# A gated MLP behind an attention block: float16 operands made ahead on GpSimd, and the gate in one pass

## The chip, the cores and the metric

The kernel runs on one core of a Trainium2 chip. The core has a matrix engine (TensorE, PE in the profile), three engines for element-wise work (VectorE, DVE; ScalarE, ACT; GpSimd, POOL), and SyncE (SP), which here does nothing but issue DMA transfers. TensorE reads its operands from the on-chip memory SBUF and writes to the accumulation memory PSUM. Each engine takes its instructions in the order in which they are queued, and semaphores make an instruction wait for work on other engines. The metric is the device time of one execution in microseconds (us).

## The reference

The input x has 2048 rows of 512 float32 numbers. First comes attention with 32 heads of 16 columns, then a gated MLP in which a 2048 x 2048 matrix mixes the rows:

```python
h  = x + softmax_attention(layernorm(x) @ wqkv) @ wo      # 32 heads, 16 columns each
z  = gelu_tanh(layernorm(h) @ w_in)                       # 2048 x 1376
z1 = z[:, :688]
z2 = layernorm(z[:, 688:])                                # 2048 x 688
g  = w_sp @ z2 + b_sp[:, None]                            # w_sp: 2048 x 2048
out = h + (z1 * g) @ w_out                                # w_out: 688 x 512
```

Everything is float32. The kernel keeps the accuracy by splitting an operand into a high part and a low part (the rest) and by multiplying high x high, high x low and low x high: three matmuls for one, in the helper `mm3` (lines 93 to 96).

## The kernel before

The work has four stages, one after another.

*Start.* Rows of x are normalized, turned, and multiplied by wqkv; q, k and v go to DRAM, q and k as float16 parts.

*Attention.* The loop runs over 512 units (group of four heads, block of 512 queries, block of 128 keys), two units an iteration. For each iteration TensorE makes the scores (line 660), ScalarE takes their exponential (L663), and TensorE multiplies by v (L671). So that the exponential does not overflow, the largest score of every query is found ahead: `max_pair` (lines 192 to 239) makes the scores of 128 queries a second time, eight steps an iteration, and VectorE takes their maximum (L215, L224). Eight iterations make a group g; at its end VectorE joins the maxima (nm, L230), GpSimd splits them into two parts (L233 to L235), and in the next iteration VectorE turns them (`max_rows`, L246), after which SP writes them into the query tile as extra rows. The group is needed by the scores some four iterations after its end. GpSimd also clears a part of the tile mx for each group (L203), copies v (L170), and splits wo and w_in into parts (`load_weights`, six times).

*z stage.* For 16 blocks of 128 rows, in the order 0, 1, 8, 9, 2, 10, 3, 11 and so on, so that a row block of the top half is followed by its partner of the bottom half: the attention's output o times 1/sum (GpSimd, L600), times wo (`make_h`), layernorm, turn (`turn`, L843), times w_in in four tiles of 344 columns with twelve matmuls each (`make_z`), gelu (L858), layernorm of the right half (`gate_z`, L864 to L888). All these operands are float32 parts.

*Gate stage.* w_sp @ z2 is done by Strassen's scheme in Winograd's form: w_sp is cut into four quarters a11, a12, a21, a22, z2 into b11, b12 (top rows, left and right columns) and b21, b22; seven products of sums of quarters (s1 to s4, t1 to t3, n4) replace eight. Each product takes, for one block p of 128 rows out of eight, 8 x 3 = 24 matmuls of 344 columns. It runs in two passes over p. The first pass (four products: s3 x t3, s2 x t2, a22 x n4, s1 x t1) loads w_sp, makes the sums on VectorE (`difference`, `sums`) and the parts on ScalarE and VectorE (`put`, L788 and L789), and sends results to DRAM (g_scr). Then b21 and b22 take the place of t2 and t3. The second pass makes the other three (a11 x b11, s4 x b22, a12 x b21), adds the stored results and the bias (L1153), multiplies by z1, turns the product (`Out.turn`, L1117) and multiplies it by w_out, whose 688 rows are five blocks of 128 and one of 48: 18 matmuls of 512 columns for each 128 rows of the output.

The order of instructions on each engine is that of the program text inside `manual_schedule`; in attention GpSimd is not in that list, and a planner places its instructions. SP's queue is one line of DMA issues for all loads and for most stores.

Of the kernel before, what the change touches and what calls it, by code (L numbers as in the profile page):

```python
# [12 lines left out]
I32 = mybir.dt.int32  # L13
# [31 lines left out]
EIGHT_OVER = float(257 << 23)  # L45


@with_exitstack
def block_kernel(ctx: ExitStack, tc: tile.TileContext, x, wqkv, wo, w_in, w_sp4, b_sp, w_out, out):
# [29 lines left out]
    z_scr = [dram.tile([S, FH], F32, name=f"z{i}_scr") for i in range(2)]  # L79
    s_scr = dram.tile([HB, P, HB, P], F32, name="s_scr")  # L80
    g_scr = [dram.tile([3, P, FC], F32, name=f"g{p}_scr") for p in range(HB)]

    def split(hi, lo, src, eh=None, el=None):

        if eh == "act":
            nc.scalar.activation(hi, src, AF.Copy)  # L86
        elif eh == "pool":
            nc.gpsimd.tensor_copy(hi, src)
        else:
            nc.vector.tensor_copy(hi, src)  # L90
        (nc.gpsimd if el == "pool" else nc.vector).tensor_sub(lo, src, hi.bitcast(F32))

    def mm3(ps, lh, ll, rh, rl, first, last):
        nc.tensor.matmul(ps, lh, rh, start=first, stop=False)  # L94
        nc.tensor.matmul(ps, lh, rl, start=False, stop=False)  # L95
        nc.tensor.matmul(ps, ll, rh, start=False, stop=last)  # L96

    def rstd_of(pool, var, n, between=lambda: None):

        hv = pool.tile([P, n], F32, name=f"rs_v{n}")  # L100
        nc.vector.tensor_scalar(hv, var, EPS, 0.5, op0=ALU.add, op1=ALU.mult)
# [62 lines left out]
    def load_v(hg):  # L164
# [5 lines left out]
        nc.gpsimd.tensor_copy(  # L170
# [84 lines left out]
    with ExitStack() as pre:  # L255
# [190 lines left out]
        with tc.manual_schedule(engines={E.PE, E.Activation, E.DVE, E.SP}):  # L446
# [95 lines left out]
            for j in range(24):  # L542
# [18 lines left out]
                if j == 4:  # L561
                    load_v(0)
# [19 lines left out]
    wi2 = [ec.tile([P, DB, 2 * FH], F32R, name=f"wi{i}") for i in range(2)]  # L582
# [36 lines left out]
    def scale_h(sb):  # L619
        mv = e2.tile([P, 2], F32, name="mv")  # L620
        nc.vector.bn_aggr(mv, hst.pop(sb))
        return mv, rstd_of(e2, mv[:, 1:2], 1)
# [19 lines left out]
    with ExitStack() as at:  # L642
# [44 lines left out]
        def load_weights(i):  # L687

            t = wc.tile([P, DB * D], F32, name="wg", tag="w0")
            if i < 2:  # L690
                t = t[:, :2 * D].rearrange("p (a c) -> p a c", a=2)
                a, f = slice(2 * i, 2 * i + 2), slice(0, D)
                src, dst = wo4, wo2
            else:
                t = t[:, :2 * FH].rearrange("p (a c) -> p a c", a=2)
                b = FH * (i // 4)
                a, f = slice(i % 2 * 2, i % 2 * 2 + 2), slice(b, b + FH)
                src, dst = wi4, wi2
            nc.sync.dma_start(t, src[:, a, f])
            split(dst[0][:, a, f], dst[1][:, a, f], t, "pool", "pool")  # L700
# [3 lines left out]
        with tc.manual_schedule(engines={E.PE, E.Activation, E.DVE, E.SP}):  # L704
            for n in range(0, len(units), 2):
                (hg, qb, kb), (_, _, kb1) = units[n:n + 2]
                if hg + 1 < HG and n % 64 < 24 and n % 4 == 0:
# [3 lines left out]
                if hg + 1 < HG and n % 64 == 30:  # L711
                    load_v(hg + 1)
# [36 lines left out]
                if n % 32 == 16 and n < 6 * 32:  # L749
                    load_weights(n // 32)  # L750
# [19 lines left out]
    T = {n: [zc.tile([P, HB, FC], F32R, name=f"{n}_{i}") for i in range(2)]  # L770
         for n in ("t3", "t2", "n4", "t1")}
    QB = HB // 2

    class Slot:


        def __init__(self, pool, tag):
            self.pool, self.tag = pool, tag

        def take(self):  # L780
            t = self.pool.tile([P, 2, HB, P], F32R, name="ws", tag=self.tag)
            return t[:, 0], t[:, 1]

    def parts(hi, lo, src, el=None, eh=None):
        if eh == "pool":
            nc.gpsimd.tensor_copy(hi, src)
        else:
            nc.scalar.activation(hi, src, AF.Copy)  # L788
        (nc.gpsimd if el == "pool" else nc.vector).tensor_sub(lo, src, hi.bitcast(F32))  # L789

    def load_a(halves, i, j, p):

# [434 lines left out]
```

## Time and profile before

| | |
|---|---|
| time, median of 3 runs | 1839.71 us (1837.95 to 1841.82) |
| profiled execution | 1840.91 us, span 1839.0 us |
| TensorE clock granted, mean | 0.995 |
| busy: PE, DVE, ACT, POOL | 97%, 84%, 72%, 11% of the span |
| attention, to its last score product | about 1350 us |
| z stage | about 1356 to 1528 us |
| gate stage | 1528 to 1839 us |

The profile's page gives sums over the whole span; stretches of time, groups of equal instructions and single instructions are read from the trace. In a row of a group, the part after the first bar is the busy time in us and the mean duration of one instruction in ns; after the second bar stands how long the engine had been idle before such instructions and what ended that. In a row of the timeline the first number is the start in us, the second the duration. A name such as `g<-t,ws` is the tile written and the tiles read. PEld is the loading of a matmul's stationary operand.

### The profile page before, as it was taken

How to read it: one execution, taken by the hardware profiler on the slowest of the kernel's cores; microseconds unless marked ns; L12 is line 12 of the kernel's file. 1: busy time of each engine (PE TensorE's matmuls, PEld its weight loads, DVE VectorE, ACT ScalarE, POOL GpSimd, SP SyncE). 2: the span in 40 equal slices, each digit the busy share in tenths (PEclk: the TensorE clock that was granted, in tenths of full speed). 3: DMA queues.
4: the chain of work that ended last, by engine and by line, in shares of the span. 5: the costliest groups of instructions: out<-in, count | busy, mean ns of one | idle time of the engine just before them, and what ended most of it. 6: DMA issues, size and time to landing. Idle time of an engine off the chain costs nothing.

```text
span 1839.0 us, 32468 instructions
## 1 busy us (share of the span) xinstructions
PE 1787.3 (97%) x11616; PEld 857.3 (47%) x11616; DVE 1552.4 (84%) x3137; ACT 1332.4 (72%) x1733; POOL 210.1 (11%) x322
## 2 busy tenths in 40 slices
PE   8999999999999999999999999999989999999999
PEld 6766222222222222222222222222259998998887
DVE  6578999999999999999999999999447778776554
ACT  3333999999999999999999999999954434343221
POOL 2121001011010000000000000000005551001121
PEclk9999999999999999999999999999999999999999
DMA  5343110120021001001011011000135555567551
GB/s 170 118 120 100 41 23 20 28 45 24 22 46 30 22 17 22 23 22 21 14 32 21 9 30 28 9 9 8 45 88 166 165 167 191 185 211 235 177 181 69
DMA packets 148105, 135.90 MB, mean 74 GB/s; under 512 B 62952, under 2 KB 108088, under 8 KB 147944
## 3 DMA queue, kind: packets, MB, share of 16 engines
q1 hardware_dynamic: 143304, 122.56, 23.9%
q10 hardware_dynamic: 4608, 11.27, 1.6%
q8 instruction: 91, 1.49, 0.3%
q14 instruction: 70, 0.57, 0.1%
q0 software_dynamic: 32, 0.01, 0.0%
HBM read 87.01 MB, written 46.17 MB: 72 GB/s over the span
## 4 chain that ended last, share of the span: by engine, by line
PE 67%; ACT 18%; issue 9%; DVE 4%; DMA 2%; SPq 0%; ACTq 0%; POOL 0%; DVEq 0%; POOLq 0%
PE pv L671 18%; PE m L210 13%; ACT pt L663 12%; PE s L660 6%; PE acc L94 6%; PE acc L96 6%; PE acc L95 6%; ACT ab L220 5%; PE g L94 3%; PE g L96 3%; PE g L95 3%; DVE mx L215 1%; PE tp L1117 1%; DMA rc<-r_scr 0%; DMA b<-z_scr 0%
## 5 line engine op out<-in xcount | busy, mean ns | idle before, releaser
L663 ACT ACTIVATE pt<-s 128x1024 f32<-128x1024 f32 x1024 | 996.3, 1038 | 72.3 <-PE s L660 68.8
L215 DVE TENSOR_REDUCE mx<-m 128x1 f32<-128x512 f32 x1511 | 965.5, 684 | 26.3 <-PE m L210 10.2
L671 PE MATMUL pv<-pt,vst 128*32 128x512 f32 x4096 | 551.9, 605 | 0.8 <-ACT o L678 0.8
L210 PE MATMUL m<-kst,qst 48*128 48x512 f16 x1511 | 479.4, 379 | 18.8
L660 PE MATMUL s<-qst,kst 50*128 50x512 f16 x2048 | 418.2, 379 | 2.0 <-DVE mx L215 0.6
L210 PEld LDWEIGHTS <-qst 48*128 48x128 f16 x2048 | 147.2, 94 | 538.9 <-issue 504.6
L660 PEld LDWEIGHTS <-kst 50*128 50x128 f16 x2048 | 144.2, 94 | 150.7 <-issue 73.3
L210 PE MATMUL m<-uvs,qst 48*128 48x512 f16 x503 | 191.3, 381 | 0.0
L224 DVE CUSTOM_DVE_ANT_0 ab<-m,ab 128x512 f32<-128x512 f32 x252 | 171.6, 681 | 3.4 <-ACT ab L220 2.7
L671 PEld LDWEIGHTS pv<-pt,vst 128*32 128x32 f32 x4096 | 83.1, 108 | 182.9 <-issue 167.7
L220 ACT ACTIVATE ab<-m 128x512 f32<-128x512 f32 x251 | 151.6, 604 | 14.4 <-PE tp L210 9.9
L233 POOL TENSOR_SCALAR nm<-nm 128x16 f32<-128x16 f32 x32 | 6.5, 204 | 842.9 <-DVE nm L230 842.9
L788 ACT ACTIVATE ws<-a 128x512 fp32r<-128x512 f32 x80 | 45.8, 621 | 57.7 <-issue 37.9
L94 PE MATMUL acc<-wi,hT 128*128 128x344 f32 x256 | 83.1, 325 | 0.0
L96 PE MATMUL acc<-wi,hT 128*128 128x344 f32 x256 | 81.8, 320 | 0.0
L95 PE MATMUL acc<-wi,hT 128*128 128x344 f32 x256 | 81.7, 319 | 0.0
L858 ACT ACTIVATE z<-acc 128x344 f32<-128x344 f32 x64 | 28.8, 456 | 55.9 <-PE acc L96 55.8
L789 DVE TENSOR_TENSOR ws<-a,ws 128x512 fp32r<-128x512 f32 x80 | 56.8, 751 | 10.2 <-ACT ws L788 10.1
L94 PE MATMUL g<-b,ws 128*128 128x344 f32 x192 | 65.0, 339 | 0.0
L86 ACT ACTIVATE pT<-tp 128x384 fp32r<-128x384 f32 (+2 forms) x48 | 18.3, 382 | 64.4 <-PE tp L1117 47.2
L94 PE MATMUL g<-t,ws 128*128 128x344 f32 x192 | 61.6, 321 | 3.3 <-ACT p L1034 2.0
L95 PE MATMUL g<-b,ws 128*128 128x344 f32 x192 | 61.9, 322 | 0.0
(197 smaller groups left out, 2163.8 us busy)
## 6 DMA issues: line engine op xcount, KB each, us to landing
a<-in_w_sp SPq DMA_DIRECT2D x80, 256.0 KB
z_scr<-z ACTq DMA_DIRECT2D x32, 344.0 KB
qst<-q_scr SPq DMA_DIRECT2D x192, 32.0 KB
kst<-k_scr SPq DMA_DIRECT2D x48, 128.0 KB
z<-z_scr SPq DMA_DIRECT2D x14, 344.0 KB
b<-z_scr SPq DMA_DIRECT2D x24, 172.0 KB
g_scr<-q SPq DMA_DIRECT2D x24, 172.0 KB
xg<-in_x SPq DMA_DIRECT2D x16, 256.0 KB
```

The source lines that it names most:

```text
L94: nc.tensor.matmul(ps, lh, rh, start=first, stop=False)
L95: nc.tensor.matmul(ps, lh, rl, start=False, stop=False)
L96: nc.tensor.matmul(ps, ll, rh, start=False, stop=last)
L210: nc.tensor.matmul(acc, q[r, p, c], keys[r, p], start=True, stop=True)
L215: nc.vector.reduce_max(at(t, e if t else e - 1), acc, axis=AX.X)
L220: nc.scalar.activation(ab[0], acc, AF.Abs)
L224: nc.vector.tensor_tensor_reduce(ab[0], acc, ab[0], 0.5, LOW, ALU.add, ALU.max, at(0, 0))
L660: nc.tensor.matmul(s[:, t, :], k[r, p, kb * P:(kb + 1) * P], q[r, p, :], start=True, stop=True)
L663: nc.scalar.activation(t, s, AF.Exp, scale=scales_[hg // 2])
L671: nc.tensor.matmul(pv[0][32 * j:32 * j + 32, :], vst[hg % 2][:, c:c + 32], pts[j % 2][:, j // 2, :], start=kb == 0, stop=kb == NB - 1)
L788: nc.scalar.activation(hi, src, AF.Copy)
L789: (nc.gpsimd if el == "pool" else nc.vector).tensor_sub(lo, src, hi.bitcast(F32))
```

## The change

- w_in, the normalized rows that meet it, z2's blocks and w_sp's operands become float16 parts instead of float32 parts. So that float16 can hold them, w_in and w_sp are multiplied by powers of two, taken from a bound on their size, and the layernorms by fixed ones (`HN_UP`, `Z2_UP`); the gelu's scale and w_out take them out again. wo and w_out stay float32 parts.
- GpSimd makes all of these operands during attention, in small steps ("chores"): it adds up absolute values of w_in and w_sp (`magnitude`), VectorE takes the maximum and derives the powers of two (`measure_weights`, `figure`), then GpSimd splits wo and w_in (`split_piece`), w_out (`out_piece`), and makes a11, a12, a22 and s1 to s4 for all of w_sp (`quarters`), which go to DRAM (op_scr). Loads and stores of the chores are issued on SP by `upon`. GpSimd is now in the list of `manual_schedule` in attention, so its order is the program's. The copy of v on GpSimd stands three iterations after its load.
- In the z stage all seven z2 operands b11, b21, b22, t1, t2, t3, n4 are made as they come, by ScalarE, VectorE and GpSimd, and stay in SBUF; z2 itself no longer goes to DRAM. Eight operand tiles of w_sp are asked for in the last eight row blocks.
- The gate is one pass: for each p seven products into three PSUM tiles, accumulating (A: b11, then t2, t3, n4; C: t1, then b22; B: b21), then z1, turn and w_out. Nothing of the gate goes to DRAM in between.
- The 48 last rows of w_out: the turned product's last block holds the last 64 columns twice, its lower half being replaced by the low part, so that two matmuls do what three did (`multiply`): 17 for 18.

```diff
+        def work(k):
+            for _ in range(k):
+                i = done_[0]
+                for fn in upon.pop(i, ()):
+                    fn()
+                if i < len(chores):
+                    chores[i]()
+                done_[0] += 1
...
+        def magnitude(key, pieces, cols):
+            acc = wp.tile([P, cols], F32, name=f"acc_{key}")
...
+                def double(got=got, two=two):
+                    two.append(wp.tile([P, 512], F32, name="two", bufs=2)[:, :cols])
+                    pool.tensor_scalar(two[0], got[0], 0.0, 2.0, op0=ALU.max, op1=ALU.mult)
+                def absolute(got=got, two=two, n=n):
+                    pool.tensor_sub(two[0] if n else acc, two[0], got[0])
+                steps = [double, absolute]
+                if n:
+                    steps.append(lambda two=two: pool.tensor_add(acc, acc, two[0]))
+                job(load, steps, 12)
+        def measure_weights():
+            top = wp.tile([P, 2], F32, name="top")
+            for i, key in enumerate(("sp", "in")):
+                nc.vector.tensor_reduce(top[:, i:i + 1], sizes_of[key], axis=AX.X, op=ALU.max)
+            nc.sync.dma_start(top_scr.rearrange("o (p i) -> (o p) i", i=2), top)
+            tops.append(wp.tile([P, 2 * P], F32, name="tops"))
+            nc.sync.dma_start(tops[0], top_scr.to_broadcast([P, 2 * P]))
+        def figure():
+            low = wp.tile([P, 2], F32, name="low")
+            nc.vector.tensor_reduce(low, tops[0].rearrange("q (p i) -> q i p", i=2), axis=AX.X, op=ALU.max)
...
+        def split_piece(src, by, hi, lo, cols):
+            got, load = piece(src, cols=cols)
+            steps = [lambda: pool.tensor_copy(hi, got[0]),
+                     lambda: pool.tensor_sub(lo, got[0], hi if hi.dtype == F16 else hi.bitcast(F32))]
+            if by is not None:
+                steps.insert(0, lambda: times(got[0], by))
+            job(load, steps, 12)
...
+        def quarters(p, c):
...
+                def high():
+                    t.append(wp.tile([P, 2, 512], F16, name="op", bufs=5))
+                    pool.tensor_copy(t[0][:, 0], of())
+                chores.append(high)
+                chores.append(lambda: pool.tensor_sub(t[0][:, 1], of(), t[0][:, 0]))
+                soon(len(chores) + LATER, lambda: nc.sync.dma_start(
+                    op_scr[p][name][:, :, k0:k0 + 4, :], t[0].rearrange("p i (k t) -> p i k t", t=P)))
...
+            job(load, [lambda: times(a[1, 0], up), lambda: times(a[1, 1], up), first_sum], 20)
+            both("s1", lambda: a["s"])
+            chores.append(lambda: times(a[0, 0], up))
+            both("a11", lambda: a[0, 0])
...
+        magnitude("in", [wi4[:, d, f] for d, f in in_pieces], FC)
+        magnitude("sp", [w_sp4[t][:, 4 * k:4 * k + 4, :].rearrange("p k t -> p (k t)")
+                         for t in range(NB) for k in range(4)], 512)
+        soon(len(chores) + 1, measure_weights)
+        for d in range(DB):
+            split_piece(wo4[:, d, :], None, wo2[0][:, d, :], wo2[1][:, d, :], 512)
+        soon(len(chores), figure)
...
-        with tc.manual_schedule(engines={E.PE, E.Activation, E.DVE, E.SP}):
+        with tc.manual_schedule(engines={E.PE, E.Activation, E.DVE, E.Pool, E.SP}):
             for n in range(0, len(units), 2):
                 (hg, qb, kb), (_, _, kb1) = units[n:n + 2]
+                if m % 8 < 6 and n < 480:
+                    work(5)
...
             if sb < HB:
+                b1, b2 = z[1][:, :FC], z[1][:, FC:]
+                parts("b11", sb, b1, "act", "pool")
+                nc.gpsimd.tensor_sub(b1, b2, b1)
+                parts("t1", sb, b1, "pool", "pool")
                 return
...
+            e.tensor_sub(t2, b22, t1)
+            parts("t2", k, t2, eh, el)
+            parts("b22", k, b22, "act", el)
+            nc.gpsimd.tensor_sub(b12, b22, b12)
+            parts("t3", k, b12, "pool", "pool")
+            parts("b21", k, b21, "act", None)
+            e.tensor_sub(t2, b21, t2)
+            parts("n4", k, t2, eh, el)
...
+                if k >= NB - 8:
+                    ask()
...
+        def product(acc, b, start=True):
+            a = ring.pop(0)
+            for k in range(HB):
+                mm3(acc, a[:, 0, k, :], a[:, 1, k, :], T[b][0][:, k, :], T[b][1][:, k, :],
+                    start and k == 0, k == HB - 1, skip_group_check=True)
+            ask()
...
+                product(A, "b11")
+                nc.scalar.activation(p1, A, AF.Identity, bias=bt)
+                if p:
+                    before[0].multiply(everything)
+                    before[0].store()
+                product(C, "t1")
+                nc.scalar.activation(q5, C, AF.Identity, bias=bb)
+                if p:
+                    before[1].turn(0, 1)
+                    before[1].split(0, 1)
+                product(A, "t2", False)
+                nc.scalar.activation(v, A, AF.Identity, bias=bt)
+                if p:
+                    before[1].multiply(everything)
+                    before[1].store()
+                product(C, "b22", False)
+                nc.vector.tensor_add(right, C, v)
+                nc.gpsimd.tensor_mul(right, right, z1t[:, FC:])
+                nc.gpsimd.tensor_copy(top.pr[:, FH:], top.pr[:, FH - TW:FH])
+                product(A, "t3", False)
+                nc.vector.tensor_add(br, A, q5)
+                nc.gpsimd.tensor_mul(br, br, z1b[:, FC:])
+                nc.gpsimd.tensor_copy(bot.pr[:, FH:], bot.pr[:, FH - TW:FH])
+                product(B, "b21")
+                nc.vector.tensor_add(left, B, p1)
+                (nc.vector if last else nc.gpsimd).tensor_mul(left, left, z1t[:, :FC])
...
+                product(A, "n4", False)
+                nc.vector.scalar_tensor_tensor(bl, A, bb, z1b[:, :FC], op0=ALU.add, op1=ALU.mult)
+                top.turn(0, 1)
+                top.split(0, 1)
```

More of the change, by code (lines that the diff above doesn't have):

```diff
@@ L810, in half @@
[L810 to L830 removed]
+    fs = ctx.enter_context(tc.tile_pool(name="fs", bufs=9, side="right"))
@@ L832, in block_kernel, with ask @@
+    T = {n: [zc.tile([P, HB, FC], F16, name=f"{n}_{i}") for i in range(2)]
+         for n in ("b11", "b21", "b22", "t1", "t2", "t3", "n4")}
+    queue = [(p, n) for p in range(HB) for n in TAKEN]
+    ring = []
+    def ask():
+        if queue:
+            p, n = queue.pop(0)
+            t = fs.tile([P, 2, HB, P], F16, name="op")
+            nc.sync.dma_start(t, op_scr[p][n])
+            ring.append(t)
     with ExitStack() as mid:
```

502 lines of the change are left out of this document (191 added, 311 removed).

## The prediction

> **What bounds the kernel now.** I read the page first, then busy time by stage, then the waits of the gate stage, then single rows of the timeline for the distance from one instruction to the next.
>
> ```profile
> span 1839.0 us, 32468 instructions
> ...
> core 0: us, PE busy (x) PEld busy (x) DVE busy (x) ACT busy (x) POOL busy (x), PEclk, DMA share, GB/s
> 600.00:800.00 200.00, 196.60 (x1406) 51.66 (x1399) 196.22 (x374) 188.09 (x225) 5.07 (x25) 1.00 0.10 21
> 1340.00:1360.00 20.00, 12.41 (x71) 3.69 (x65) 3.21 (x8) 10.37 (x13) 2.54 (x2) 0.86 0.34 85
> 1440.00:1500.00 60.00, 60.00 (x362) 57.27 (x362) 45.24 (x149) 26.27 (x46) 32.69 (x39) 1.00 0.58 170
> ```
>
> The three stretches are attention, its end, and the z stage. In attention TensorE, VectorE and ScalarE are all at 94 to 98%, and GpSimd works 5 us in 200: work put on GpSimd there is free as long as nobody waits for it, and work put on VectorE costs its length. In the z stage, and in the gate stage after it, TensorE alone is full. Busy matmul time overlaps, so the price of a matmul is the distance between starts, here in the timeline:
>
> ```profile
> 707.87 0.39 PE L210 MATMUL m<-kst,qst 48*128 48x512 f16 x1
> ...
> 708.52 0.39 PE L660 MATMUL s<-qst,kst 50*128 50x512 f16 x2
> ...
> 1502.14 0.39 PE L95 MATMUL acc<-wo,o 128*128 128x512 f32 x1
> ...
> 1503.73 0.39 PE L96 MATMUL acc<-wo,o 128*128 128x512 f32 x1
> ...
> 1504.56 0.32 PE L95 MATMUL acc<-wi,hT 128*128 128x344 f32 x1
> ...
> 1511.80 0.32 PE L96 MATMUL acc<-wi,hT 128*128 128x344 f32 x1
> ```
>
> Float32 parts: 512 columns, 7 steps in 1.59 us, 227 ns each; 344 columns, 46 steps in 7.24 us, 157.4 ns. That is 0.414 ns a column and some 15 ns besides. Float16 at 512 columns: 3 steps in 0.65 us, 217 ns, so only some 5 ns besides.
>
> **The gate stage** has a steady beat, read from one ScalarE instruction in each pass (L1034 in the first, L1154 in the second):
>
> ```profile
> 1585.69 0.44 ACT L1034 ACTIVATE p<-g 128x344 f32<-128x344 f32 x1
> ...
> 1630.83 0.44 ACT L1034 ACTIVATE p<-g 128x344 f32<-128x344 f32 x1
> ...
> 1704.82 0.55 ACT L1154 ACTIVATE pr<-g,bias 128x344 f32<-128x344 f32 x1 [1.80 <-DVE pr L1153]
> ...
> 1813.84 0.55 ACT L1154 ACTIVATE pr<-g,bias 128x344 f32<-128x344 f32 x1 [1.80 <-DVE pr L1153]
> ```
>
> Three beats of the first pass take 45.14 us (15.05 each: 4 products of 24 matmuls), five of the second 109.02 us (21.80 each: 3 products and two row blocks of w_out). Eight of each are 294.8 us. The ends of the stage, and two rows of TensorE's waits:
>
> ```profile
> 1528.28 0.39 PE L94 MATMUL g<-t,ws 128*128 128x344 f32 x1 [0.64 <-ACT z L858]
> ...
> 1834.72 0.39 PE L96 MATMUL acc<-wu,pT 128*128 128x512 f32 x1
> ```
> ```profile
> PE tp L1117 <- DVE pr L1155: 4.3, 1, 4.3
> PE g L94 <- ACT p L1034: 2.0, 1, 2.0
> ```
>
> The gate's first matmul starts at 1528.3 after a wait of 0.6, so z ended near 1527.6; to 1839.0 are 311.4 us, 16.6 above the beats. From the slot after the last matmul (1834.95) to the end are 4.05 us, for y and its store. The other 12.6 lie at the start, where products wait for the last T blocks and operands, and between the passes (4.3).
>
> **The change, step by step.** *Matmuls in float16.* z has 64 tiles of 12 matmuls, 768; the gate 8 x 7 x 24 = 1344, as many as before. By the steps each saves 227 - 217 = 10 ns; the ends are 0 (if full 128-row float16 matmuls step like float32 ones, which no row excludes) and 15 (no fixed part). I take 10.5: 8.1 us in z, 14.1 in the gate. The Trainium skill ("TensorE: Matmul & The Clock Gate", Back-to-back issue gap) gives columns / 2.4 GHz + 2.5 ns for a warm array: 216 ns at 512, with which the float16 steps agree and which the float32 steps exceed. By it 344 columns would be 146 ns, an estimate, and the saving 24 us in all.
>
> *w_out in 17 products.* The last block of 48 rows is three matmuls now:
>
> ```profile
> 1749.26 0.40 PE L96 MATMUL acc<-wu,pT 128*128 128x512 f32 x1
> ...
> 1750.49 0.42 PE L94 MATMUL g<-b,ws 128*128 128x344 f32 x1
> ```
>
> From the slot after 1749.26 (1749.49) to the next product at 1750.49 is 1.00 us; two full matmuls are 0.45. Saved: 0.55 x 16 = 8.8 us. GpSimd's added copies of 64 columns lie under products.
>
> *One pass.* Between passes there is nothing left to wait for. The first products read b11 and t1, made from the top rows well before; t2, some 4 us late by ScalarE's and VectorE's work after the last gelu, is needed two products (7 us) in. What is late next is the PSUM bank at the start (0.6). I leave 2.5 of the 12.6, so 10.1 saved; ends 6 and 12. Operands are asked for 8 products ahead, 28 us.
>
> *z stage beside TensorE.* The operand sums leave ScalarE and VectorE, which had 26 and 45 of 60 us; GpSimd's prices:
>
> ```profile
> L789 POOL TENSOR_TENSOR t<-z,t 128x344 fp32r<-128x344 f32 x14 | 13.0, 928 | 1.1
> L786 POOL CAST t<-t 128x344 fp32r<-128x344 f32 x7 | 3.3, 471 | 0.0
> L600 POOL TENSOR_TENSOR o<-o,rc 128x512 f32<-128x512 f32 x16 | 20.6, 1286 | 119.4 <-DMA rc<-r_scr 106.2 <-DVE nb L626 8.8 <-DVE rs_t L111 4.4
> ```
>
> A pair of rows has ten two-input operations, four casts and two products o*rc: 9.3 + 1.9 + 2.6 = 13.8 us of some 20.5; hidden. Operand loads of 512 KB now stand before o and rc on SP's queue in rows 8 to 11: 1.0 us against the change.
>
> *GpSimd's chores in attention.* By the code there are 47 + 191 + 8 + 48 + 18 + 352 = 664 (sizes of w_in and w_sp, wo, w_in, w_out, 16 pieces of the quarters with 22 each), in groups of 30: five in each of six iterations, none in two; so 22 groups of 32. VectorE's maximum nm closes a group of eight iterations:
>
> ```profile
> 643.17 0.20 POOL L233 TENSOR_SCALAR nm<-nm 128x16 f32<-128x16 f32 x1 [35.82 <-DVE nm L230]
> ...
> 679.75 0.20 POOL L233 TENSOR_SCALAR nm<-nm 128x16 f32<-128x16 f32 x1 [35.82 <-DVE nm L230]
> ...
> 646.63 0.21 DVE L246 STREAM_TRANSPOSE mturned<-mparts 128x32 f16<-128x32 f16 x1
> ```
> ```profile
> L91 POOL TENSOR_TENSOR wi<-wg,wi 128x1376 fp32r<-128x1376 f32 x4 | 12.5, 3115 | 0.3
> L233 POOL TENSOR_SCALAR nm<-nm 128x16 f32<-128x16 f32 x32 | 6.5, 204 | 842.9 <-DVE nm L230 842.9
> L394 POOL TENSOR_TENSOR part<-uv,part 128x512 f16<-128x512 f32 x4 | 4.7, 1168 | 0.3
> L294 POOL TENSOR_SCALAR each<-ident,most 128x128 f32<-128x128 f32 x8 | 3.0, 373 | 7.1 <-DVE most L290 6.9
> L393 POOL CAST part<-uv 128x512 f16<-128x512 f32 x4 | 2.4, 609 | 0.3
> ```
>
> A group lasts 36.58 us, an iteration 4.57. Queued behind the chores are nm and its parts (0.7 us with the memset), and VectorE's transpose, which comes some 2.7 us after the parts, waits for them. So GpSimd must finish a group's chores within 35.9 us. A tensor_scalar over 512 columns is not in the trace. Below lies the one-input cast, 0.61; above, L294 in proportion, 1.49; the line through L233 and L294 gives 0.96. I take 0.80, between the cast and the line, which are nearest in kind. The costliest stretch is the size of w_sp, whose pieces are one tensor_scalar and two two-input operations (1.29, L600): a group is 10 x (0.80 + 2.58 + 0.16 for dependent starts) + 0.7 = 36.1 us and just fits. The 22 chores of such a piece are 4 x 0.80 + 4 x 1.29 + 7 x (0.61 + 1.17) + 1.0 = 21.8 us, so 30 take 30. On SP, stores that wait for a lagging GpSimd hold up the q and k loads for 2 us at most, and those are asked for an iteration or more ahead. The chores' transfers are some 68 MB in 22 groups (805 us), 84 GB/s on top of 21; the z stage moves 170 at a share of 0.58.
>
> *What VectorE pays there, once.* It measures the sizes, priced by its nearest rows:
>
> ```profile
> L290 DVE TENSOR_REDUCE most<-wg 128x1 f32<-128x512 f32 x8 | 5.1, 676 | 0.0
> L305 DVE TENSOR_REDUCE low<-tp 128x2 f32<-128x256 f32 x4 | 1.7, 419 | 2.9 <-PE tp L303 2.9
> ```
>
> The maximum over w_sp's sizes stands in VectorE's queue at chore 239, in the third iteration of a group, two iterations (9.15 us) after nm. Thirteen chores of that group must be done by then: 0.7 + 1.29 + 4 x 3.54 = 16.2 us. VectorE waits 7.0 us, and TensorE and ScalarE behind it (ends 2 and 14). The reductions (0.68, 0.45, 0.42) and six small instructions are 2.6 us. The load of the two figures is hidden by the two iterations between. After the idle stretch at 1340:1360 above the granted clock was 0.86 over 20 us, 2.8 us of missing pulses; I put half of that, 1.4, on the restart. Together 11.0 us.
>
> **The sum:** 8.1 + 14.1 + 8.8 + 10.1 = 41.1 saved, 1.0 + 11.0 = 12.0 lost, 29.1 net. The profiled execution took 1840.9 us (span 1839.0), 1.2 above the median of 1839.7; 1840.9 - 29.1 - 1.2 = 1810.6, so 1811. With the ends above its own range is 1797 to 1826.
>
> **Rivals.** *GpSimd becomes the bound (the other side).* If a tensor_scalar costs 1.49, a group of w_sp's size takes 43.0 us, 6.4 too long, and VectorE waits at the transpose in each of 6.4 groups: 41 - 2.7 = 38 us, 1849, slower. It decides from 1.34 us (a group of 41.5) on. The cast at 0.61 speaks against it.
>
> *Contention between GpSimd and VectorE.* The same form cost GpSimd twice as much in one place of the gate stage; in attention, VectorE worked alike with GpSimd busy (first stretch) and idle (second):
>
> ```profile
> L1167 POOL TENSOR_TENSOR pr<-pr,z 128x344 f32<-128x344 f32 x7 | 12.2, 1736 | 46.9 <-issue 40.1 <-DVE pr L1166 6.8
> L1185 POOL TENSOR_TENSOR pr<-pr,z 128x344 f32<-128x344 f32 x6 | 5.6, 926 | 34.8 <-DVE pr L1184 34.8
> ```
> ```profile
> 448.50:452.90 4.40, 3.67 (x7) 1.00 0.06 16
> 485.10:489.50 4.40, 3.67 (x7) 1.00 0.30 75
> ```
>
> If two-input chores took 1.87 times as long in attention, a w_sp group would be 59 us and a group of the quarters 46: some 270 us over 22 groups, near 2080. The wi row speaks against it: 3115 ns in attention, 2.26 a column, where L600 pays 2.51. The Trainium skill ("GPSIMD Engine Reference", Key points) has GpSimd contend with VectorE instructions in a two-port mode or with two SBUF inputs; by that rule attention, whose VectorE reads PSUM, is spared, and the trace agrees (3.67 us in both stretches).
>
> *The memset of mx, now behind five chores.* It ends some 6.4 us after nm. If VectorE's writes of the second iteration (5.2 us after nm) waited for it, 1.2 x 22 groups = 26 us, 1837. They write other elements of the tile, and no row shows such a wait.
>
> *Float16 brings nothing:* 22 us less, 1833.
>
> **Chances.** Forecast 0.67; GpSimd bound 0.12, of which a little over half above 1843; contention 0.05; memset 0.06, half of it slower; float16 nothing 0.06; more saved than the range 0.04. About 0.2% (3.7 us) is what a measurement here can tell from no change. Faster 0.82, same 0.03, slower 0.15. The range 1797 to 1842 leaves out the slower cases and the better one.
>
> **What would show it.** Right: 344-column steps of 146 to 148 ns in z and gate; a gate beat near 34 us; groups of 36.6 us in attention but for one of some 47; GpSimd two-input chores at 1.17 to 1.29 us. Wrong: idle time of VectorE before L246's transpose in group after group, SP waiting for GpSimd, TensorE waiting for operands or for a first product after z.

## The result and the profile after

The changed kernel takes 1882.97 us (median of 4 runs, 1880.35 to 1883.11) against 1840.7 us for the kernel before on the same chip: a ratio of 1.0229, 95% interval 1.0211 to 1.0246. It is slower, by 42 us; I had forecast 1811. The profiled execution has a span of 1881.0 us, so the two spans differ by 42.0 us as well, and the stages add up to that. Each stage is read between two instructions that both kernels have: the last maximum nm of attention, the first and the last turn of a row block in the z stage, the first product of the gate.

| stage, us | before | after | difference | forecast |
|---|---|---|---|---|
| start to the last nm | 1301.67 | 1378.14 | +76.5 | +11.0 |
| last nm to first turn | 48.24 | 53.66 | +5.4 | 0 |
| first to last turn (z) | 162.05 | 159.30 | -2.8 | -7.1 |
| last turn to first gate product | 16.32 | 15.32 | -1.0 | in the next row |
| gate to the end | 310.72 | 274.58 | -36.1 | -33.0 |

The gate gave what it was to give, and more. Attention took all of it back, twice over. First two lists of the page of the kernel after: busy tenths in 40 slices, and the chain that ended last.

```profile
PE   9999998888869999999999999999998999999999
...
DVE  6488997777759999999999999999933687211112
...
POOL 2131999999974787787687500000001566201010
PEclk9999998988879999999999999999998999999999
...
PE 56%; POOL 17%; ACT 13%; issue 7%; DVE 4%; DMA 1%; SPq 1%; ACTq 0%; POOLq 0%; DVEq 0%
```

GpSimd stands at 9 in slices 5 to 11. In slices 5 and 6 VectorE and TensorE are still full; in slices 7 to 11 VectorE is at 7 and TensorE at 8, and in slice 12 both are lower still. From slice 13 on GpSimd has air and both are full again. The chain runs 17% of its length over GpSimd, an engine that worked 11% of the span before. The same in stretches of 200 us (columns: stretch, length, then busy us and instructions of PE, PEld, DVE, ACT, POOL, then granted clock, DMA share, GB/s), kernel after:

```profile
200.00:400.00 200.00, 176.50 (x1191) 45.59 (x1188) 167.41 (x317) 161.33 (x193) 188.05 (x156) 0.93 0.29 76
400.00:600.00 200.00, 162.49 (x1076) 41.41 (x1079) 153.00 (x295) 145.00 (x172) 168.05 (x155) 0.88 0.25 67
600.00:800.00 200.00, 196.43 (x1403) 51.32 (x1396) 195.74 (x373) 188.18 (x225) 145.27 (x183) 1.00 0.46 129
```

The first two rows are mostly the measurement of the sizes of w_in and w_sp (185 to 541 us), the third the making of w_in, w_out and the quarters. In the third, with GpSimd busy for 145 us, VectorE works 195.7 of 200 as it did before (196.2): GpSimd's work as such disturbs nobody there. What differs is in its groups (by form: us busy in all, mean ns):

```profile
L746 POOL TENSOR_SCALAR two<-raw 128x512 f32<-128x512 f32 x64 | 122.9, 1920 | 0.0
...
L749 POOL TENSOR_TENSOR two<-two,raw 128x512 f32<-128x512 f32 x63 | 80.2, 1272 | 4.9
L753 POOL TENSOR_TENSOR acc_sp<-acc_sp,two 128x512 f32<-128x512 f32 x63 | 80.1, 1271 | 4.5
...
L732 POOL TENSOR_SCALAR raw<-raw,figs 128x512 f32<-128x512 f32 x64 | 44.1, 696 | 0.0
```

L732 (times a power of two, written as two multiplications) takes 0.70 us, a little under the 0.80 that I had put for every tensor_scalar. L746, a maximum and a multiplication on the same 512 columns, takes 1.92. With that a group of w_sp's size is 10 x (1.92 + 2.55 + 0.16) + 0.7 = 47.0 us of chores in a period of 36.6. The timeline of VectorE, at the maximum that closes each group:

```profile
276.42 0.22 DVE L237 TENSOR_REDUCE nm<-mx 128x16 f32<-128x64 f32 x1
...
323.16 0.22 DVE L237 TENSOR_REDUCE nm<-mx 128x16 f32<-128x64 f32 x1
...
415.84 0.22 DVE L237 TENSOR_REDUCE nm<-mx 128x16 f32<-128x64 f32 x1
...
462.95 0.22 DVE L237 TENSOR_REDUCE nm<-mx 128x16 f32<-128x64 f32 x1
...
572.34 0.22 DVE L237 TENSOR_REDUCE nm<-mx 128x16 f32<-128x64 f32 x1
...
609.00 0.22 DVE L237 TENSOR_REDUCE nm<-mx 128x16 f32<-128x64 f32 x1
```

276.42 to 323.16 is 46.7 us, 415.84 to 462.95 is 47.1, and 572.34 to 609.00, the first group without sizes, 36.7. From 276 to 572 us six groups are together 76 us longer than 36.6 us each (five by some 10, and the one in which VectorE takes its maximum over the sizes by 26). The waits between 150 and 1340 us (us in total, times, longest) show the path by which GpSimd's lag reaches TensorE:

```profile
PE m L217 <- DVE mx L222: 55.9, 8, 12.9
DVE mturned L253 <- POOL mparts L242: 47.2, 6, 8.3
...
DVE top L760 <- POOL acc_sp L753: 12.7, 1, 12.7
```

VectorE's transpose waits 8 us in each of six groups for nm's parts, which stand behind the chores; TensorE then waits for VectorE to free a PSUM bank. GpSimd itself has no idle time ahead of the six scalings of nm that are late (286.9 to 520.7 us), and from each to the next are 46.5 to 47.5 us, the 47.0 of the chores. So its chores set the length of the first five groups; in the sixth VectorE waits 12.7 us more, for the last sum ahead of its maximum. TensorE's granted clock goes down in the same groups (third number from the end), here in one of them and in the first without sizes:

```profile
415.84:462.95 47.11, 39.61 (x260) 10.05 (x256) 36.03 (x69) 34.78 (x42) 45.38 (x36) 0.89 0.32 76
...
572.34:609.00 36.66, 36.01 (x260) 9.49 (x264) 35.88 (x69) 34.50 (x42) 19.13 (x34) 1.00 0.29 82
```

The lower clock goes along with the waits; no run here shows that it makes the groups longer than GpSimd does.

The 5.4 us at the end of attention are another matter. GpSimd and then VectorE there, in the kernel after:

```profile
1383.95 1.27 POOL L610 TENSOR_TENSOR o<-o,rc 128x512 f32<-128x512 f32 x1 [41.28 <-DMA rc<-r_scr]
1385.19 0.20 POOL L240 TENSOR_SCALAR nm<-nm 128x16 f32<-128x16 f32 x1
...
1386.00 0.21 DVE L253 STREAM_TRANSPOSE mturned<-mparts 128x32 f16<-128x32 f16 x1 [7.63 <-POOL mparts L242]
```

The last maximum was there at 1378.36, but its scaling on GpSimd now stands, in program order, behind o*rc of the first z row, which waits for a DMA until 1383.95.

### The profile page after: what moved, and what is told of

Same layout as the page of the kernel before. It is cut to its first block, busy times and chain, and to the rows that moved or that the text cites. A ratio compares the mean times of both kernels' runs of the same rounds, so it can differ in the third digit from the quotient of the medians.

```text
span 1881.0 us, 33006 instructions
## 1 busy us (share of the span) xinstructions
PE 1777.2 (94%) x11600; PEld 733.7 (39%) x11600; DVE 1408.1 (75%) x2906; ACT 1275.5 (68%) x1607; POOL 900.0 (48%) x1014
## 3 DMA queue, kind: packets, MB, share of 16 engines
q8 instruction: 91, 1.49, 0.3%
## 4 chain that ended last, share of the span: by engine, by line
PE 56%; POOL 17%; ACT 13%; issue 7%; DVE 4%; DMA 1%; SPq 1%; ACTq 0%; POOLq 0%; DVEq 0%
PE pv L681 14%; PE m L217 10%; ACT pt L673 9%; POOL two L746 6%; PE acc L101 5%; PE acc L103 5%; PE acc L102 5%; PE s L670 5%; POOL two L749 4%; POOL acc_sp L753 4%; ACT ab L227 4%; PE g L101 3%; PE g L103 3%; PE g L102 3%; DVE mx L222 2%
## 5 line engine op out<-in xcount | busy, mean ns | idle before, releaser
L681 PE MATMUL pv<-pt,vst 128*32 128x512 f32 x4096 | 560.2, 614 | 0.0
L217 PE MATMUL m<-kst,qst 48*128 48x512 f16 x1511 | 488.5, 384 | 31.3 <-DVE mx L222 13.3
L670 PE MATMUL s<-qst,kst 50*128 50x512 f16 x2048 | 431.9, 386 | 5.9 <-DMA qst<-mturned 3.7
L746 POOL TENSOR_SCALAR two<-raw 128x512 f32<-128x512 f32 (+1 forms) x80 | 144.7, 1808 | 11.2 <-PE s L670 11.2
L1102 ACT ACTIVATE pT<-tp 128x384 fp32r<-128x384 f32 x32 | 14.0, 488 | 142.0 <-PE tp L1094 142.0
L749 POOL TENSOR_TENSOR two<-two,raw 128x512 f32<-128x512 f32 (+1 forms) x78 | 93.9, 1204 | 6.0
L826 POOL TENSOR_TENSOR op<-raw,op 128x512 f16<-128x512 f32 x80 | 92.8, 1160 | 6.2
L610 POOL TENSOR_TENSOR o<-o,rc 128x512 f32<-128x512 f32 x16 | 20.4, 1274 | 147.6 <-DMA rc<-r_scr 96.8
L753 POOL TENSOR_TENSOR acc_sp<-acc_sp,two 128x512 f32<-128x512 f32 x63 | 80.1, 1271 | 4.5
L101 PE MATMUL acc<-wi,hT 128*128 128x344 f16 x256 | 79.1, 309 | 0.0
L102 PE MATMUL acc<-wi,hT 128*128 128x344 f16 x256 | 79.1, 309 | 0.0
L103 PE MATMUL acc<-wi,hT 128*128 128x344 f16 x256 | 79.1, 309 | 0.0
```

The costliest lines, as they stand in the source:

```text
L101: nc.tensor.matmul(ps, lh, rh, start=first, stop=False, **kw)
L102: nc.tensor.matmul(ps, lh, rl, start=False, stop=False, **kw)
L103: nc.tensor.matmul(ps, ll, rh, start=False, stop=last, **kw)
L217: nc.tensor.matmul(acc, q[r, p, c], keys[r, p], start=True, stop=True)
L670: nc.tensor.matmul(s[:, t, :], k[r, p, kb * P:(kb + 1) * P], q[r, p, :], start=True, stop=True)
L681: nc.tensor.matmul(pv[0][32 * j:32 * j + 32, :], vst[hg % 2][:, c:c + 32], pts[j % 2][:, j // 2, :], start=kb == 0, stop=kb == NB - 1)
```

## The experiments

**One operation of GpSimd changed, with fixed figures on VectorE (multmult).**

```diff
-                    pool.tensor_scalar(two[0], got[0], 0.0, 2.0, op0=ALU.max, op1=ALU.mult)
+                    pool.tensor_scalar(two[0], got[0], 2.0, 1.0, op0=ALU.mult, op1=ALU.mult)
...
-            nc.vector.tensor_scalar(low, low, 2.0 ** -53, None, op0=ALU.max)
+            nc.vector.memset(low[:, 0:1], 2.0 ** -3)
+            nc.vector.memset(low[:, 1:2], 2.0)
```

> The 80 tensor_scalars of the size measurement are (2x times 1), two multiplications, in place of max(x, 0) times 2; their number, place and tiles are the same, and the figures are fixed (2^-3 and 2), so the size of the weights is left out of what is computed. Theory (the price of max-and-multiply alone, 1920 ns where I had taken 800, makes GpSimd late): the operation takes about 0.70 us as the other tensor_scalars of the kernel after, a w_sp group is 10 x (0.70 + 2.55 + 0.16) + 0.7 = 34.8 us, under the 36.6 us of a group, attention loses nothing, and the time is 1883 - 76 = 1807 us (1803 to 1812). Rival (the mass of added work on GpSimd, its SBUF traffic or its place in the order, whatever its operations): groups of 45 us and more remain, 1865 us or more.

Measured: 1814.72 us (1814.51 to 1817.36), ratio 0.9857 (0.9840 to 0.9873): 68 us faster than the kernel after, with as many instructions on GpSimd in the same places. Its group of the same operation, the longest of VectorE's waits between 459 and 510 us, and the one long group by VectorE's maximum:

```profile
L746 POOL TENSOR_SCALAR two<-raw 128x512 f32<-128x512 f32 x64 | 39.7, 620 | 0.0
```
```profile
DVE top L760 <- POOL acc_sp L753: 6.5, 1, 6.5
```
```profile
459.90 0.22 DVE L237 TENSOR_REDUCE nm<-mx 128x16 f32<-128x64 f32 x1
...
507.01 0.22 DVE L237 TENSOR_REDUCE nm<-mx 128x16 f32<-128x64 f32 x1
```

The operation takes 0.62 us, and all groups but one last 36.6 us. The one, 47.1 us, holds VectorE's maximum over the sizes, waiting 6.5 us where I had worked out 7.0. The time is 8 above the expected 1807 because I had forgotten these 10.5 us in that expectation; the rival (1865 or more) is out. The price of one kind of instruction is the cause of the loss in attention.

**The same work thinner (spread3).**

```diff
-                    work(5)
+                    work(3 if done_[0] < sized else 5)
```

> As the kernel after, max-and-multiply kept and the size measured, but three chores instead of five in each iteration as long as the size is measured; the later chores move back. Theory (what counts is the length of a group's chores against the group's 36.6 us): 18 chores are 6 x (1.92 + 2.55 + 0.16) + 0.7 = 28.5 us, GpSimd is never late, 1807 us (1803 to 1815). Rival (the sum of GpSimd's work in attention, 80 x 1.92 us and all else, is paid by VectorE wherever it lies): about as the kernel after, 1870 us or more.

Measured: 1813.70 us (1812.71 to 1815.34), ratio 0.9853 (0.9837 to 0.9870). The operation still takes 1920 ns, its 64 and 16 instructions still 144.6 us, and nobody pays for them. So GpSimd's load in sum costs nothing; a group whose chores are longer than the group does. What remains above 1807 is again VectorE's maximum and figures: two groups of 42.2 and 40.1 us, 9.1 together.

**What makes it dear (forms, forms2).** The tensor_scalar of the size in eight forms, four in turn in each run (one execution of each run):

```diff
-                    pool.tensor_scalar(two[0], got[0], 0.0, 2.0, op0=ALU.max, op1=ALU.mult)
+                    if n % 4 == 0:
+                        pool.tensor_scalar(two[0], got[0], 0.0, 2.0, op0=ALU.max, op1=ALU.mult)
+                    elif n % 4 == 1:
+                        pool.tensor_scalar(two[0], got[0], 2.0, 0.0, op0=ALU.mult, op1=ALU.max)
+                    elif n % 4 == 2:
+                        pool.tensor_scalar(two[0], got[0], 2.0, 0.0, op0=ALU.mult, op1=ALU.add)
+                    else:
+                        pool.tensor_scalar(two[0], got[0], 0.0, None, op0=ALU.max)
```

> The tensor_scalar of the size measurement in four forms in turn: max then mult, mult then max, mult then add, and max alone (with fixed figures, so the size is left out of what is computed). Theory 1 (max itself is dear on GpSimd): the three forms with max take 1.5 to 1.9 us at 512 columns, mult and add 0.7. Theory 2 (two different operations in one instruction are dear): mult and add 1.9 too, max alone 0.7. Theory 3 (max ahead of another operation): only the first 1.9. By theory 1 w_sp groups are about 10 x (1.6 + 2.55 + 0.16) + 0.7 = 43.8 us and the time near 1855; by 2 near the same; by 3 near 1812.

> best2 with the tensor_scalar of the size measurement in four other forms in turn: min then mult, is_gt then mult, one mult alone, max then min (fixed figures, so the size is left out of what is computed). If every comparison is dear on GpSimd (some 1.3 us each at 512 columns above a multiplication): min and is_gt with mult 1.9, mult alone 0.5 to 0.62, max with min 2.5 or more. If max alone is dear: min and is_gt with mult 0.62, max with min 1.9. At three chores an iteration the time stays that of best2, 1803.5 (1801 to 1806), in either case.

Groups of the run forms, by form (L747 is max then mult, L749 mult then max, L751 mult then add, L753 max alone):

```profile
L747 POOL TENSOR_SCALAR two<-raw 128x512 f32<-128x512 f32 x16 | 30.8, 1925 | 0.0
...
L749 POOL TENSOR_SCALAR two<-raw 128x512 f32<-128x512 f32 x16 | 30.9, 1930 | 0.0
...
L751 POOL TENSOR_SCALAR two<-raw 128x512 f32<-128x512 f32 x16 | 9.9, 618 | 0.0
L751 POOL TENSOR_SCALAR two<-raw 128x344 f32<-128x344 f32 x4 | 1.9, 480 | 0.0
...
L753 POOL TENSOR_SCALAR two<-raw 128x512 f32<-128x512 f32 x16 | 23.9, 1493 | 0.0
```

And of forms2 (L752 min then mult, L754 is_gt then mult, L756 mult alone, L758 max then min):

```profile
L752 POOL TENSOR_SCALAR two<-raw 128x512 f32<-128x512 f32 x16 | 30.9, 1934 | 0.0
L754 POOL TENSOR_SCALAR two<-raw 128x512 f32<-128x512 f32 x16 | 30.9, 1929 | 0.0
...
L756 POOL TENSOR_SCALAR two<-raw 128x512 f32<-128x512 f32 x16 | 24.0, 1501 | 0.0
L756 POOL TENSOR_SCALAR two<-raw 128x344 f32<-128x344 f32 x4 | 4.3, 1080 | 0.0
...
L758 POOL TENSOR_SCALAR two<-raw 128x512 f32<-128x512 f32 x16 | 30.8, 1926 | 0.0
```

The first run looked like "max is dear" (theory 1). The second refutes this, since min and is_gt cost as much as max. It refutes "every comparison is dear" too, since a single multiplication costs as much as a single maximum, and two comparisons cost no more than one with a multiplication. What stands in the rows are three classes: two arithmetic operations 0.62 us, one operation of either kind 1.50, a pair with a comparison 1.93. By the rows at 344 and 512 columns a column costs (618 - 480) / 168 = 0.82 ns in the first class and (1501 - 1080) / 168 = 2.5 ns in the second. The times were 1854.1 us for forms (five chores an iteration; expected 1855) and 1803.9 for forms2 (built on best2, below; expected 1803.5). Why the classes are so isn't shown.

**The order at the end of attention (nmfirst, before_pool).** In the kernel after, the first o*rc is put behind the last maximum:

```diff
-                if n in (486, 490, 506):
+                if n == 486:
+                    first_o = load_o(h_rows[0], True)
+                if n == 490:
+                    first_o()
+                if n in (490, 506):
                     load_o(h_rows[min((n - 486) // 4, 2)])
```

> As the kernel after, but GpSimd's product o times rc of the first row of the z stage is issued after the last group's maximum nm and not ahead of it. Theory (the maximum stands behind a product that waits for rc's DMA): the transpose of the last group no longer waits 7.6 us, the first turn of the z stage comes 5.7 us sooner, 1877 us. Rival (the z stage needs that product just as soon, so the wait only moves): the same time as the kernel after, 1883 us.

Measured: 1874.49 us (1873.67 to 1876.24), ratio 1.0182 (1.0165 to 1.0199). From the last nm to the first turn are 48.2 us again, as before the change, instead of 53.7; the transpose waits 0.89 us. By the profiles 2.3 us more lie ahead of the last nm (1375.84 for 1378.14), where the code is the same; I don't put them down to the edit. The counterpart, in the kernel before:

```diff
-        with tc.manual_schedule(engines={E.PE, E.Activation, E.DVE, E.SP}):
+        with tc.manual_schedule(engines={E.PE, E.Activation, E.DVE, E.Pool, E.SP}):
```

> The kernel before with GpSimd too in program order through the attention, nothing else. Theory (in program order the last group's maximum stands behind the first product o times rc, which waits for a DMA until 1307 us): about 6 us slower, 1847 (1845 to 1849). Rival (the order costs nothing there, and the 8.5 us that the reordered kernel won are particular to the kernel after): 1841.

Measured: 1844.7 us against 1839.8, ratio 1.0033 (1.0021 to 1.0046), 4.9 us slower; last nm to first turn is 53.3 us instead of 48.2. Its timeline:

```profile
1306.21 1.28 POOL L600 TENSOR_TENSOR o<-o,rc 128x512 f32<-128x512 f32 x1 [41.17 <-DMA rc<-r_scr]
1307.45 0.20 POOL L233 TENSOR_SCALAR nm<-nm 128x16 f32<-128x16 f32 x1
...
1308.26 0.21 DVE L246 STREAM_TRANSPOSE mturned<-mparts 128x32 f16<-128x32 f16 x1 [7.52 <-POOL mparts L235]
```

One word in the list of engines costs 5 us, in either kernel (in the kernel before I had expected 6): the planner had been placing nm ahead of a product that was not yet ready.

**The three repairs together (best2).** spread3 and nmfirst, and VectorE's maximum two chores later:

```diff
-        soon(len(chores) + 1, measure_weights)
+        sized = len(chores)
+        soon(len(chores) + 3, measure_weights)
```

> The kernel after with three changes of order and none of the work: three chores instead of five per iteration while the size is measured, GpSimd's first product o times rc after the last maximum, and VectorE's reduction of the sizes two chores later, so that the sums it reads are done. If the three gains add: 1813.7 (three chores) - 8.5 (the order, 1883.0 to 1874.5) - 4 (of the 9.1 us that the two groups with the reduction and the figures are longer, 3.5 are VectorE's own operations and 2.5 its wait, the rest stalls behind it) = 1801 us (1798 to 1805), faster than both kernels by more than 2%. If the reduction costs its own operations only, without the wait being paid: 1805.

Measured: 1803.47 us (1802.62 to 1804.30), ratio to the kernel before 0.9806 (0.9793 to 0.9818). It is faster than the kernel before, by 1.9% (the more than 2% that I had expected isn't shown), and faster than the kernel after, whose work it does in another order. VectorE reads the sizes without a wait, where spread3 had one of 2.46 us, and the two groups around it are 37.3 and 40.3 us long instead of 42.2 and 40.1. Attention ends 3.0 us behind the kernel before.

**w_out in 18 products again (w18).** On best2:

```diff
-                        c = i * P if i < WB else FH - TW
-                        nc.tensor.transpose(tp[:, i - i0, :], self.pr[:, c:c + P], ident)
+                        f0, n = FB[i]
+                        nc.tensor.transpose(tp[:n, i - i0, :], self.pr[:, f0:f0 + n], ident)
...
-                        nc.tensor.matmul(self.acc, hi[:, i, :], wu5[0], start=a, stop=False)
-                        nc.tensor.matmul(self.acc, hi[:, i, :], wu5[1], start=False, stop=z)
+                        mm3(self.acc, hi[:fn, i, :], lo[:fn, i, :], wu5[0], wu5[1], a, z)
```

> As best2, but the last 48 rows of w_out are three matmuls of 48 rows again (18 products per row block, with their own transpose, one more copy on ScalarE and one more subtraction on VectorE; GpSimd's copies of 64 columns are gone). Theory (w_out's rows are paid by TensorE alone, 1.00 us for the three where two full ones take 0.45): 16 x 0.55 = 8.8 us above best2, 1810 (1808 to 1812), and a gate beat of 34.9 us. Rival (the product's price lies in the wait for its transposes and splits, so that the number of matmuls matters little): within 3 us of best2.

Measured: 1810.32 us (1809.51 to 1812.78), ratio to the kernel before 0.9841 (0.9827 to 0.9856), 6.9 above best2 by the medians and 9.5 by the spans of the profiles, of which 8.5 lie in the gate stage (283.1 for 274.6). The gate's beat in best2, then in w18, five beats apart:

```profile
1589.84 0.55 ACT L1174 ACTIVATE p<-g,fig 128x344 f32<-128x344 f32 x1 [2.91 <-PE g L103]
...
1758.67 0.55 ACT L1174 ACTIVATE p<-g,fig 128x344 f32<-128x344 f32 x1 [2.91 <-PE g L103]
```
```profile
1591.85 0.55 ACT L1172 ACTIVATE p<-g,fig 128x344 f32<-128x344 f32 x1 [2.05 <-PE g L103]
...
1765.95 0.55 ACT L1172 ACTIVATE p<-g,fig 128x344 f32<-128x344 f32 x1 [2.05 <-PE g L103]
```

168.83 / 5 = 33.77 us against 174.10 / 5 = 34.82: 1.05 us a beat, 0.53 for each row block, where the step of the prediction was 0.55.

**What the z stage waits for (inv0, inv_early).** In both, on best2, the reciprocal of the last head group's sums is moved forward:

```diff
-                if k == 1:
+                if k == 0:
                     invert()
```

> As best2, but the reciprocals of the last head group's sums are taken in the first row of the z stage, not the second. Theory (the z stage won 3 us and not 8 since its fifth row waits for a chain of fixed length, reciprocal, store, rc's load, product, which float16 doesn't shorten): that row comes after 10.2 us, not after 14 to 16, and the time is 4 us below best2, 1797 (1795 to 1799). Rival (that row waits for another thing of the same chain, o's own load or ScalarE's split): best2's time.

Measured: 1804.06 us (1800.80 to 1806.33), best2's time: the rival's number. From the reciprocal to the next product o*rc are 12.0 us in best2 (1382.46 to 1394.44, for the sixth row block of the stage, whose products with wo stand ahead of the fifth turn) and 12.1 in inv0 (1374.08 to 1386.14, for the fifth row block, ahead of the fourth turn): the store of the reciprocals now stands on SP's queue ahead of the loads of the row before, so that this row waits in its place. By the code neither row block uses these reciprocals: they belong to queries 1536 to 2047, the sixth row block is rows 1280 to 1407 of x and the fifth rows 256 to 383. What ties them is the order of SP's queue, in best2:

```profile
1382.73 1.72 SPq L652 DMA_DIRECT2D r_scr<-rcp  x4
1384.54 0.38 SPq L603 DMA_DIRECT2D o<-o_scr  x1
```

SP waits 5.2 us for VectorE ahead of the store, and the loads of o and rc stand behind it. Loads put ahead of the store were not tried.

Then the reciprocal ahead of the first row's products:

```diff
                     nb = minus_mean(e2, mv, rs)
+                if k == 0:
+                    invert()
                 new_z(sb)
```

> As best2, but the last reciprocals of the sums stand ahead of the first row's z products (and not behind them as in the run inv0, where the store and rc's loads also put the row before them off, so that the wait only moved). In both runs the reciprocal and the product o times rc that hangs on it lie 12.0 us apart. Theory (that chain of 12 us is what the z stage waits for, by its start alone): reciprocal near 1364 us, product of the fifth row no later than 1386, no row of more than 11 us behind the second, 4 us below best2, 1799.5 (1797 to 1801). Rival (the rows wait for the loads of o and rc on SP's queue, which come when a row's slot comes): best2's time, 1803.5.

Measured: 1802.01 us (1800.26 to 1803.26), 1.5 below best2; the intervals against the kernel before (0.9784 to 0.9810 and 0.9793 to 0.9818) overlap, so the measured times don't tell them apart. The traces do in the stage itself: first to last turn is 156.3 us for 158.8. The reciprocal came at 1373.0, not at the 1364 expected, since VectorE reaches it only after h of a later row. TensorE's wait for the row block whose loads stand behind the store, the sixth in best2 and the fifth in inv_early:

```profile
1396.42 0.77 PE L101 MATMUL acc<-wo,o 128*128 128x512 f32 x1 [2.14 <-ACT o L92]
```
```profile
1387.05 0.50 PE L101 MATMUL acc<-wo,o 128*128 128x512 f32 x1 [0.82 <-ACT o L92]
```

The wait is 1.3 us shorter, and the row's twelve products with wo take 3.15 us for 4.45, another 1.3. So a part of the missing z gain hangs on when this store is issued. That it would all come back with an earlier start is not shown.

## Why the prediction was wrong

*The step that failed* is the price of the tensor_scalar in "GpSimd's chores in attention": 0.80 us, with 1.49 as the upper end. The rows from which it was bounded, L233 and L294, are both two multiplications, and I took them for the price of every tensor_scalar. For those operations the number was good (0.70 measured in the kernel after, 0.62 with constants). For the 64 of 512 columns that take a maximum it was 1.92, above my upper end. The step should have asked which of the kernel's instructions share the operation, and not only the name, with the one to be priced; no row did, so that the bound upwards was open. Even the line through these two rows, 0.95 us at 512 columns (the prediction has 0.96), makes a group 37.6 us, which doesn't fit; only the choice of 0.80 below it made the term fit.

*The rival "GpSimd becomes the bound"* is what happened, by its own mechanism and at its own place: the wait shows at the transpose in six groups. It was to make the kernel slower from 1.34 us on, and its own price of 1.49 was too low for the same reason: at 1.92 a group is some 10.5 us too long and not 6.4, and the group with VectorE's maximum waits longer (12.7 for 7.0). A chance of 0.12 for a term that "just fits" (36.1 of 36.6 us) was too little: 0.05 us on each of ten operations was all the room there was.

*What VectorE pays once* (11.0 us) held: 10.5 in multmult, where GpSimd keeps up. *Order on GpSimd* was looked at for nm and the memset, not for the first z rows: 5.4 us at the end of attention that no step has. I had costed the loads of o and rc on SP (1.0) and gone past the engine that waits for them.

*Float16 in z* (8.1 us): the steps are right, and the sum was not. In the kernel after, nine steps lie between these two rows, 1.31 us:

```profile
1563.68 0.31 PE L101 MATMUL acc<-wi,hT 128*128 128x344 f16 x1
...
1564.99 0.31 PE L101 MATMUL acc<-wi,hT 128*128 128x344 f16 x1
```

That is 145.6 ns each, where float32 parts took 157.4; a row block is 10.2 us for 10.74. By the formula that the Trainium skill ("TensorE: Matmul & The Clock Gate", Back-to-back issue gap) gives for an isolated matmul on a warm array, 344 columns are 146 ns, an estimate. The trace agrees. But the stage as a whole won 2.8 us: from the first turn to the second are 13.7 us for 12.5, from the fourth to the fifth 14.8 for 12.6. In both places TensorE waits for o, whose transfers float16 doesn't shorten. In the first place it waits 7.79 us for 7.59; the second, in the kernel before and then in the kernel after:

```profile
1393.40 0.50 PE L94 MATMUL acc<-wo,o 128*128 128x512 f32 x1 [1.33 <-ACT o L86]
```
```profile
1476.43 0.50 PE L101 MATMUL acc<-wo,o 128*128 128x512 f32 x1 [2.57 <-ACT o L92]
```

The greater part is what follows the waits. The twelve products of 512 columns there, in the same two places, kernel before and then after, as stretches from the first product to the turn with the granted clock as the third number from the end:

```profile
1358.16:1362.44 4.28, 4.28 (x12) 3.25 (x13) 0.75 (x2) 0.00 (x0) 0.00 (x0) 0.64 0.00 0
1393.40:1396.55 3.15, 3.15 (x13) 2.25 (x14) 2.90 (x10) 1.70 (x4) 0.00 (x0) 1.00 0.67 182
```
```profile
1440.24:1445.53 5.29, 5.29 (x12) 3.91 (x13) 0.75 (x2) 0.00 (x0) 0.00 (x0) 0.50 0.00 0
1476.43:1481.06 4.63, 4.63 (x13) 3.33 (x14) 3.71 (x13) 2.49 (x5) 3.92 (x5) 0.63 0.43 139
```

They are 1.0 and 1.5 us longer at a lower granted clock, the waits only 0.2 and 1.2. Why the clock stays lower in the kernel after isn't shown. I had counted 64 tiles as if TensorE set the pace, at full clock, in all of them.

*Gate, w_out and one pass* held. The beat is 33.77 us for 36.85 (forecast: near 34), 3.08 less, of which w18 shows 1.05 to be w_out's and so 2.03 float16's (12.1 ns a matmul for 10.5). Eight beats are 24.6 us, and the remaining 11.5 of 36.1 are the joint of the passes and the start (10.1). *GpSimd's two-input chores* of 512 columns took 1.16 to 1.28 us as forecast, the *contention* rival is refuted by the third stretch above, and *float16 brings nothing* by the steps. For the *memset of mx* no wait shows in groups that have room: those of multmult but one are 36.6 to 36.9 us long, as in the kernel before.

With this one price put right the sum comes out near: multmult took 1814.7 us, 4 above the forecast of 1811. That it is so near is in part luck. By the stages of its profile the order on GpSimd costs 5.7 us that no term has, and z gives 3.3 us for 7.1; the gate, with 37.2 us for 33.0, makes up for somewhat less than half of it.

## What to carry to other kernels

Price an operation by a row with the same operation in it: the instruction's name and its shape aren't enough, and where no row has it, the upper end is open and the chance of the rival that hangs on it is large. Where work is hidden under a period, its sum is not the question but whether each stretch of it fits in its period, and an estimate that "just fits" is a coin toss; three chores for five made 70 us of loss vanish. When an engine is taken from a planner into program order, look at every instruction that waits for a DMA ahead of one that somebody is waiting for.

## What the runs showed of the hardware

On GpSimd, a tensor_scalar of 128x512 float32 takes 0.62 us with two arithmetic operations (mult and mult, mult and add; 0.70 where the factor is read from a tile, L732), 1.50 with one operation (mult or max), and 1.93 with a pair that has a comparison (max, min, is_gt; for max and mult in either order). A multiplication alone is thus cheaper when it is written with a second one by 1.0. The Trainium skill ("GPSIMD Engine Reference", Elementwise — side-by-side cycle accounting) gives bodies with k up to 2, which I read as at most two operations, 1.03 cycles an element, by its 1.2 GHz 0.86 ns as an estimate. The first class comes near it with 0.82 ns a column; the 2.5 of a single operation doesn't, and there the measurement decides.

The granted TensorE clock was 0.89 to 0.91 over the five groups of 45.6 to 47.1 us, in each of which TensorE was idle for 6.5 to 7.5 us at a stretch, 0.78 over the group of 63.0 us with idle stretches of 7.6 and 12.9 us, and 1.00 over the group after it, which had none. Behind an idle stretch of 7.79 us at the head of the z stage, products of 512 columns started 0.43 us apart at a granted clock of 0.50, and 0.23 us apart where the clock was 1.00 again.
